# Attention steps on one core: the exponentials issued directly behind the maxima

## The chip, the cores and the metric

One core of a Trainium2 chip runs the whole program. The metric is the device time of one execution in microseconds (us); the runs shown of the kernel before took 1231.6, 1232.68 and 1233.63 us, median 1232.68 us. The profile is of a further execution, with its own time.

## The reference

Three stages follow each other: block-causal attention over 4 batches, 8 heads, 576 positions and 64 columns, a routed mixture of 8 experts, and a dense mixture of 4 experts. Only the first is touched by the change. Cut to it:

```python
scores = scale * np.matmul(q, k.transpose(0, 1, 3, 2))
scores = np.where(block_i >= block_j, scores, -1000000000.0)
scores = scores - np.max(scores, axis=-1, keepdims=True)
attn = np.exp(scores)
attn = attn / (np.sum(attn, axis=-1, keepdims=True) + 1e-09)
out = np.matmul(attn, v)
...
h = np.maximum(xc[mask] @ w1[e], 0.0)
y[mask] = gate_w[mask, None] * (h @ w2[e])
```

## The kernel before

**Units, groups, steps.** The attention is cut into 8 units (one batch, four heads). A unit has ten groups, and one step works on one group, so a unit has steps 0 to 9, and the attention has 80 (then a tail without exponentials). Query row tiles are rt 0 (64 rows) and rt 1 to 4 (128 rows). In units 0 to 6 the groups are: step 0 rt 0, step 1 rt 1, steps 2 and 3 rt 3 (two heads each), steps 4 and 5 rt 2, steps 6 and 7 rt 4 (heads 0 and 1), steps 8 and 9 rt 4 (heads 2 and 3). Unit 7 takes them in another order (`R7`).

**The order of a step** is written out by hand in `ORD`: each letter is a small function of `attention`, called once a step. As the scheduling is manual, the order in which the functions issue instructions is the order in which each engine takes them; engines are coupled by semaphores alone. The letters:

- S: TensorE makes the scores of the *next* group into a PSUM tile `s` (pool `ps_s`, three buffers, line 280).
- M: VectorE takes the negated row maxima `m` of this group (line 289).
- E: ScalarE turns the scores into exponentials `E` (line 296); it reads `s` and `m`. It issues nothing else. When an item is complete it also puts the item on the lists `turns` and `pvs`, with the step from which it is due (`TL`, `LG`).
- D: two pieces of the operand preparation of the next unit (`split_unit`): on ScalarE the scaled `kr` (line 209), `kh` (210) and `QH` (203), in steps 1, 2 and 3; the differences on GpSimd.
- R: the gate logits of finished rows (copies `xT`, line 397, and `lgs`, line 408, on ScalarE) and the routing of a batch of row tiles (`route`: a dozen small VectorE operations, one exponential on ScalarE, line 445).
- T: the exponentials are turned (`turn`). For rt 0, 2 and 4 ScalarE copies them to `HL` in 16 bits (line 328), GpSimd makes the rest (329) and SyncE issues a transposing DMA. For rt 1 and 3 (`PE_2`) TensorE transposes into a tile `tp` of the same three-buffer pool as the scores (line 322); one step later ScalarE copies it to `eT` (line 324) and VectorE subtracts that copy (line 325). These three ScalarE copies fall into steps 4, 5 and 6 of a unit.
- V: VectorE divides results by their sums (lines 362 to 365).
- P: TensorE's products with the values (lines 354 to 356).
- U, O: loads, and other small work.

ScalarE's work of a step is therefore, before the change: D, R, T, E. VectorE's is M, D, R, T, V in both kernels.

Of the kernel before, what the change touches and what calls it, by code (L numbers as in the profile page):

```python
# [52 lines left out]
class Kernel:  # L53
# [21 lines left out]
    SPE = ("AV", "AV", "AV", "AV", "AV", "AV", "AV", "AV")  # L75
    SB = 3
    PU, W2, X2 = 4, 1, 2
    ORD = "OSMDRTVPUE"
    TL = (2, 2, 2, 2, 2, 2, 2, 1, 3, 1, 1, 3, 0, 4, 2, 2)
    LG = (8, 9, 10, 9, 10, 4, 10, 9, 5, 12, 6, 9, 4, 4, 12, 2)  # L80
    SN = 2
# [430 lines left out]
    def attention(self, scored):  # L512
# [115 lines left out]
        while s < ns or turns or pvs or evs or self.routes or self.preps or side:  # L628
            self.tail = s >= ns
            for x in self.ORT if self.tail else self.ORD:  # L630
                order[x]()
# [533 lines left out]
```

## Time and profile before

| | |
|---|---|
| median of 3 runs | 1232.68 us (1231.6 to 1233.63) |
| profiled execution: time, span | 1235.5 us, 1233.9 us |
| TensorE busy, mean granted clock | 1130.4 us (92%), 0.960 |
| ScalarE busy | 510.7 us (41%) |
| VectorE busy | 824.8 us (67%) |
| GpSimd busy | 602.7 us (49%) |

The table is over the whole span. The attention is only its first part: its first exponential starts at 11.8 us, and its last ones are done at 201 us. In the profile DVE is VectorE, ACT is ScalarE, PE is TensorE, PEld its weight loads, POOL is GpSimd. A row of the timeline has a start, a duration, and in square brackets the time for which the engine had stood idle, with what ended that. A duration includes the time until the write is acknowledged; the next instruction on the same engine starts a little before that.

### The profile page before, as it was taken

The numbers are of one execution on the slowest core, as the hardware profiler recorded it, in microseconds if no ns is written. First come the engines' busy times: TensorE is split into PE (matmuls) and PEld (weight loads), VectorE is DVE, ScalarE is ACT, GpSimd is POOL, SyncE is SP. The second block draws the span as 40 slices with busy tenths as digits, with TensorE's granted clock in tenths as the row PEclk, the third lists the DMA queues.
The fourth block names the chain that finished last, engine by engine and source line by source line (L and its number), as shares of the span: only waits on it lengthen the run. The fifth ranks groups of instructions, "written<-read, shape, count | busy, mean of one in ns | idle before, by whom it ended". The sixth has DMA issues, their size and how long they took to land.

```text
span 1233.9 us, 21146 instructions
## 1 busy us (share of the span) xinstructions
PE 1130.4 (92%) x8105; PEld 1009.7 (82%) x8105; DVE 824.8 (67%) x1312; ACT 510.7 (41%) x900; POOL 602.7 (49%) x597
## 2 busy tenths in 40 slices
PE   5888888669898789999999999999899999999998
PEld 4778887558797678999889989888788888888887
DVE  5667576576425677766677666677877767767675
ACT  5877775356424552323322323324423332233321
POOL 6968784100011065544554454546655555555552
PEclk8889899689999989999999999999999999999999
DMA  5988749799524342111111111112311111111101
GB/s 182 208 184 195 181 116 210 254 316 312 194 92 150 100 127 69 35 35 48 39 47 39 35 35 52 35 52 69 120 35 54 50 52 52 35 52 52 35 1 69
DMA packets 129882, 123.89 MB, mean 100 GB/s; under 512 B 65965, under 2 KB 98733, under 8 KB 129744
## 3 DMA queue, kind: packets, MB, share of 16 engines
q1 hardware_dynamic: 127024, 117.48, 33.1%
q0 software_dynamic: 2720, 4.64, 1.2%
q8 instruction: 79, 1.29, 0.5%
q14 instruction: 59, 0.48, 0.1%
HBM read 91.83 MB, written 19.43 MB: 90 GB/s over the span
## 4 chain that ended last, share of the span: by engine, by line
PE 45%; DVE 9%; issue 8%; DMA 5%; ACT 4%; POOL 2%; POOLq 0%; another core or an unknown queue 0%; SPq 0%; DVEq 0%; ACTq 0%
PE yp L660 9%; PE yp L662 9%; PE yp L661 8%; PE hp L661 6%; PE hp L662 6%; PE hp L660 6%; DMA xi<-XS 4%; DVE acc L980 4%; DVE tl L893 2%; ACT hh L925 2%; DVE C L918 2%; ACT vh L889 1%; POOL C L918 1%; DMA XN<-ys,xg 1%; POOL p L918 1%
## 5 line engine op out<-in xcount | busy, mean ns | idle before, releaser
L925 ACT ACTIVATE hh<-C 128x512 fp32r<-128x512 f32 (+1 forms) x128 | 87.8, 686 | 433.6 <-DVE C L918 368.8
L660 PE MATMUL yp<-vh,hh 128*128 128x512 f32 x576 | 228.9, 397 | 10.9 <-ACT hh L925 10.9
L980 DVE SCALAR_TENSOR_TENSOR acc<-yp,p,acc 128x512 f32<-128x512 f32 x270 | 196.7, 742 | 56.6 <-PE yp L662 56.6
L662 PE MATMUL yp<-vh,hl 128*128 128x512 f32 x576 | 227.8, 395 | 0.3 <-DVE hl L926 0.3
L661 PE MATMUL yp<-vl,hh 128*128 128x512 f32 x576 | 228.0, 396 | 0.0
L926 DVE SCALAR_TENSOR_TENSOR hl<-C,hh 128x512 fp32r<-128x512 f32 (+1 forms) x128 | 120.9, 945 | 116.7 <-ACT hh L925 116.7
L918 POOL TENSOR_TENSOR p<-u,p 128x384 f32<-128x384 f32 (+1 forms) x64 | 60.3, 942 | 203.5 <-ACT p L915 203.5
L662 PEld LDWEIGHTS yp<-vh,hl 128*128 128x128 f32 x576 | 108.4, 188 | 31.8 <-DVE hl L926 8.2
L660 PEld LDWEIGHTS yp<-vh,hh 128*128 128x128 f32 x576 | 109.1, 189 | 27.4 <-ACT hh L925 14.3
L918 POOL TENSOR_TENSOR C<-u,p 128x384 f32<-128x384 f32 (+1 forms) x64 | 53.3, 833 | 149.6 <-ACT p L915 96.7
L661 PEld LDWEIGHTS yp<-vl,hh 128*128 128x128 f32 x576 | 109.0, 189 | 12.3
L661 PE MATMUL hp<-xsl,th 128*128 128x256 f32 (+1 forms) x384 | 113.9, 297 | 0.0
L662 PE MATMUL hp<-xsh,tl 128*128 128x256 f32 (+1 forms) x384 | 113.7, 296 | 0.0
L660 PE MATMUL hp<-xsh,th 128*128 128x256 f32 (+1 forms) x384 | 113.6, 296 | 0.0
L915 ACT COPY p<-hp 128x256 f32<-128x256 f32 (+1 forms) x192 | 74.8, 389 | 92.9 <-PE hp L662 92.9
L918 DVE TENSOR_TENSOR C<-hp,p 128x256 f32<-128x256 f32 (+1 forms) x128 | 57.6, 450 | 52.9 <-POOL p L918 52.9
L896 POOL TENSOR_TENSOR vl<-r,vh 128x1024 fp32r<-128x1024 f32 x31 | 91.3, 2945 | 0.0
L730 POOL DMA_INDIRECT XN<-ys,xg x10 | 13.0, 1299 | 155.4 <-DVE ys L729 106.1
L893 DVE TENSOR_TENSOR tl<-t,th 128x512 fp32r<-128x512 f32 x32 | 87.0, 2719 | 0.8 <-ACT th L891 0.8
L329 POOL TENSOR_TENSOR HL<-E,HL 128x640 bf16<-128x640 f32 (+2 forms) x39 | 66.5, 1721 | 32.1 <-ACT HL L328 23.5
L296 ACT ACTIVATE E<-s,m 128x320 f32<-128x320 f32 (+4 forms) x160 | 76.0, 532 | 10.4 <-DVE m L289 9.5
L660 PE MATMUL hp<-xdh,dh 128*128 128x256 f32 (+1 forms) x256 | 76.6, 299 | 1.9 <-ACT xdh L845 1.2
(212 smaller groups left out, 3093.8 us busy)
## 6 DMA issues: line engine op xcount, KB each, us to landing
r<-in_w_dram SPq DMA_DIRECT2D x128, 512.0 KB, 4.9
XN<-x SPq DMA_DIRECT2D x18, 256.0 KB, 8.7
x<-XN SPq DMA_DIRECT2D x18, 256.0 KB, 3.1
vr<-in_v_dram SPq DMA_DIRECT2D x7, 640.0 KB, 7.2
xg<-XS SPq DMA_DIRECT2D x16, 257.0 KB, 4.5
out_dram<-acc SPq DMA_DIRECT2D x16, 256.0 KB, 2.0
qr<-in_q_dram SPq DMA_DIRECT2D x7, 576.0 KB, 6.0
kr<-in_k_dram SPq DMA_DIRECT2D x7, 576.0 KB, 6.0
```

Source lines behind the costliest of these rows:

```text
L296: nc.scalar.activation(e, views[j], AF.Exp, bias=m[:R, c:c + 1])
L329: (nc.vector if item[:2] in self.HV else nc.gpsimd).tensor_tensor(HL[:R, w:2 * w].bitcast(BF16), Et[:R, 0:w], HL[:R, 0:w], ALU.subtract)
L660: nc.tensor.matmul(out, lhsT=ah, rhs=bh, start=start, stop=False)
L661: nc.tensor.matmul(out, lhsT=ah, rhs=bl, start=False, stop=False)
L662: nc.tensor.matmul(out, lhsT=al, rhs=bh, start=False, stop=stop)
L893: V.tensor_tensor(tl[:, 0:2], t[:, 0:2], th[:, 0:2].bitcast(F32), ALU.subtract)
L896: P.tensor_tensor(vl, r2, vh.bitcast(F32), ALU.subtract)
L915: nc.scalar.copy(t, product(a, b))
L918: add = lambda e, o, x, y: e.tensor_tensor(o, x, y, ALU.add)
L925: nc.scalar.activation(hh[:, i:i + 2], C[:, i:i + 2], AF.Relu)
L926: V.scalar_tensor_tensor(hl[:, i:i + 2], C[:, i:i + 2], 0.0, hh[:, i:i + 2].bitcast(F32), ALU.max, ALU.subtract)
L980: nc.vector.scalar_tensor_tensor(a, yp, self.p[:, n, e:e + 1], a, ALU.mult, ALU.add)
```

## The change

One string: in a step the letter E moves from the last place to the place behind M. All functions stay as they are.

```diff
-    ORD = "OSMDRTVPUE"
+    ORD = "OSMEDRTVPU"
```

ScalarE's work of a step then has the order E, D, R, T. One item, rt 0 of unit 7, has a `TL` of 0; as E comes in front of T in its step now, its turning starts one step earlier.

## Rows read from the trace of the kernel before

**Rows 1.** Busy time by engine in two stretches (us from the span's start).

```profile
core 0: us, PE busy (x) PEld busy (x) DVE busy (x) ACT busy (x) POOL busy (x), PEclk, DMA share, GB/s
20.00:183.00 163.00, 140.09 (x1977) 130.58 (x1978) 108.27 (x234) 126.08 (x226) 129.47 (x102) 0.89 0.76 173
183.00:205.00 22.00, 19.63 (x365) 18.47 (x364) 16.21 (x43) 16.26 (x35) 12.87 (x11) 1.00 1.10 195
```

**Rows 2.** Groups by line, ScalarE, 20 to 183 us: busy, mean ns | idle before.

```profile
L296 ACT ACTIVATE E<-s,m 128x320 f32<-128x320 f32 (+4 forms) x128 | 61.9, 539 | 3.4 <-DVE m L289 2.5 <-DVE r L362 0.9
...
L324 ACT CAST eT<-tp 128x896 f16<-128x896 f32 (+1 forms) x21 | 18.4, 876 | 23.0 <-PE tp L322 23.0
...
L397 ACT COPY xT<-xTp 128x512 f32<-128x512 f32 x11 | 6.5, 591 | 0.9 <-PE xTp L394 0.9
L408 ACT COPY lgs<-lg 128x9 f32<-128x9 f32 x11 | 1.9, 169 | 6.4 <-PE lg L402 6.4
L445 ACT ACTIVATE rt<-rt 128x32 f32<-128x32 f32 (+1 forms) x2 | 0.5, 233 | 3.0 <-DVE rt L439 3.0
```

**Rows 3.** Waits of TensorE, 20 to 183 us: total, times, longest.

```profile
PE s L280 <- ACT E L296: 10.5, 8, 1.7
PE s L280 <- DVE eT L325: 5.5, 7, 1.3
PE tp L322 <- ACT E L296: 5.3, 9, 1.6
```

**Rows 4.** Timeline of ScalarE, steps 4 to 8 of unit 4.

```profile
116.22 0.80 ACT L324 CAST eT<-tp 128x768 f16<-128x768 f32 x1
116.90 0.96 ACT L296 ACTIVATE E<-s,m 128x320 f32<-128x320 f32 x2
...
119.71 0.91 ACT L324 CAST eT<-tp 128x896 f16<-128x896 f32 x1 [1.10 <-PE tp L322]
120.51 0.95 ACT L296 ACTIVATE E<-s,m 128x320 f32<-128x320 f32 x2
123.07 0.91 ACT L324 CAST eT<-tp 128x896 f16<-128x896 f32 x1 [1.61 <-PE tp L322]
123.88 0.73 ACT L328 CAST HL<-E 128x640 f16<-128x640 f32 x1
124.50 0.75 ACT L296 ACTIVATE E<-s,m 128x576 f32<-128x576 f32 x1
```

**Rows 5.** Timeline of VectorE over the same steps.

```profile
117.06 0.96 DVE L325 TENSOR_TENSOR eT<-tp,eT 128x768 bf16<-128x768 f32 x1 [1.58 <-ACT eT L324]
117.93 0.81 DVE L289 TENSOR_REDUCE m<-s 128x2 f32<-128x640 f32 x1
120.65 1.09 DVE L325 TENSOR_TENSOR eT<-tp,eT 128x896 bf16<-128x896 f32 x1 [1.90 <-ACT eT L324]
121.66 0.15 DVE L362 TENSOR_SCALAR r<-og 128x4 f32<-128x4 f32 x1
...
122.39 0.75 DVE L289 TENSOR_REDUCE m<-s 128x1 f32<-128x576 f32 x1
124.01 1.09 DVE L325 TENSOR_TENSOR eT<-tp,eT 128x896 bf16<-128x896 f32 x1 [0.87 <-ACT eT L324]
125.02 0.75 DVE L289 TENSOR_REDUCE m<-s 128x1 f32<-128x576 f32 x1
```

**Rows 6.** Timeline of VectorE around a routing batch, steps 0 and 1 of unit 4.

```profile
105.75 0.42 DVE L289 TENSOR_REDUCE m<-s 64x4 f32<-64x256 f32 x1
...
109.40 0.96 DVE L289 TENSOR_REDUCE m<-s 128x4 f32<-128x768 f32 x1
```

**Rows 7.** Timeline of ScalarE over the same steps.

```profile
106.10 1.15 ACT L328 CAST HL<-E 128x1152 f16<-128x1152 f32 x1
107.16 0.91 ACT L296 ACTIVATE E<-s,m 64x64 f32<-64x64 f32 x4
107.95 1.16 ACT L209 ACTIVATE kr<-kr 128x1152 f32<-128x1152 f32 x1
...
110.45 1.36 ACT L296 ACTIVATE E<-s,m 128x192 f32<-128x192 f32 x4 [0.87 <-DVE r L362]
```

**Rows 8.** Busy time in a stretch of unit 5 (columns as in rows 1).

```profile
142.00:148.00 6.00, 6.00 (x55) 5.92 (x55) 2.46 (x5) 1.92 (x4) 5.84 (x6) 0.50 0.92 275
```

**Rows 9.** Groups by line, TensorE, 142.6 to 144.2 us: seven transposes.

```profile
L322 PE MATMUL tp<-ident,E 128*128 128x128 f32 x7 | 1.7, 426 | 0.0
```

**Rows 10.** Groups by line, TensorE, 93.8 to 94.8 us: seven transposes.

```profile
L322 PE MATMUL tp<-ident,E 128*128 128x128 f32 x7 | 1.0, 280 | 0.2 <-ACT E L296 0.2
```

## The prediction

> **What bounds the kernel now.** The edit touches the 80 steps of the attention alone, so I read the busy time of that stretch before anything else: from 20 to 183 us, which is six and a half units, TensorE is busy for 140.1 of 163 us, GpSimd for 129.5, ScalarE for 126.1, VectorE for 108.3 [rows 1]. No engine is full; the stretch is paced by how they wait for one another. The only order that the edit changes is that of ScalarE, and its work stays the same. That gives a simple account: the moment at which ScalarE has done its work up to a given step moves by exactly as much as its idle time before that step changes. Its idle time is 163 − 126.1 = 36.9 us now.
>
> The groups by line say what it waits for: 23.0 us ahead of the copies from `tp` until TensorE has transposed, 6.4 ahead of `lgs` and 0.9 ahead of `xT`, also for TensorE, 3.4 ahead of exponentials and 3.0 ahead of the routing's exponential for VectorE [rows 2]. Together 36.7, so nearly all of the 36.9 is explained. The reader is to see that the exponentials themselves hardly wait (3.4 us for 128): their maxima are long done when ScalarE comes to them, as D, R and T stand in between. What they do is to wait behind other work; TensorE pays for that with 10.5 us ahead of scores and 5.3 us ahead of transposes, where a PSUM tile is free only after an exponential [rows 3].
>
> **The change part by part.** *What moves.* E issues nothing but ScalarE's activations, one to four a step. They pass the D, R and T work on ScalarE and nothing else: E has no DMA, and puts nothing on SP's or POOL's queue. Now every ScalarE copy of a step stands behind that step's maxima. Its wait for `m` is the wait that is added to those copies.
>
> *What is gained.* An exponential of step s starts up to one step's copies earlier, and so do the scores that take its PSUM tile. Of TensorE's waits, 10.5 + 5.3 = 15.8 us [rows 3] hang on that. But TensorE's time is gained for the end only if it paces the units. ScalarE's waits for TensorE, 23.0 + 6.4 + 0.9 = 30.3 us [rows 2], should go too, since an earlier E(4) and E(5) let the transposes of steps 4 and 5 start earlier. I take all 30.3 as gone.
>
> *What is added.* In steps 4, 5 and 6 ScalarE copies a `tp`, and VectorE, in its order M, T, V, subtracts that copy before it comes to the next step's maxima. Today ScalarE does E(s) meanwhile. After the change E(s) lies behind it, and the next thing on its queue is E(s+1), which needs M(s+1), which stands behind that subtraction. The clock times of unit 4 give the price, as VectorE's three pieces keep their lengths:
> - Step 4 to 5: ScalarE is free 116.90 [rows 4]; the subtraction starts 117.06, the maxima start 117.93 and take 0.81 [rows 5], and 0.03 more reaches ScalarE: 118.77. Wait 1.87 us.
> - Step 5 to 6: free 120.51 [rows 4]; subtraction 120.65, the division of V, maxima 122.39 + 0.75 [rows 5]: 123.17. Wait 2.66 us.
> - Step 6 to 7: the `HL` copy follows, so free only 124.50 [rows 4]; subtraction 124.01, maxima 125.02 + 0.75 [rows 5]: 125.80. Wait 1.30 us.
>
> That is 5.83 us a unit. Seven units have this pattern in the stretch; the first has no results to divide in step 5, which saves 122.39 − 121.66 = 0.73 [rows 5]. Sum 7 × 5.83 − 0.73 = 40.1 us.
>
> *Routing batches.* Two fall into the stretch. The routing's own wait of 3.0 us stays [rows 2]. In unit 4 its VectorE work stands between M(0) and M(1): M(1) ends 109.40 + 0.96 = 110.36, 4.19 us behind the end of M(0), 106.17 [rows 6]. ScalarE has E(0), issue to issue 107.95 − 107.16 = 0.79, and one `HL` copy, 1.06, to fill this after the change, and waits 2.34; now it has `kr` and `xT` as well and waits 0.87 [rows 7]. So +1.5, and I take the same for the other batch, an estimate: 0 to 3 us for each. The waits of exponentials that exist now, 3.4, turn into the ones counted here; only the 0.9 at the routing stays.
>
> *ScalarE's idle time after:* 40.1 + 3.0 + 0.9 + 3.0 = 47.0 us, against 36.9: **10.1 us later** at 183 us.
>
> *What is behind that.* From 183 to 205 us TensorE is busy for 19.6 of 22 us [rows 1]. It enters this stretch with less unfinished work when ScalarE is late, so it can win back something between nothing and its 2.4 us of idle time; I take 1.5. Everything after the attention (routing of the last rows, weights, both mixtures) follows from its end, and I shift it unchanged. GpSimd's copies from `HL` and `QH` come about a microsecond later in their step; their results are needed several steps on, and it has 33.5 us free [rows 1], so I cost this at nothing; were GpSimd to fall behind, products would wait, at up to about 1 us a unit (an estimate, from the size of an exponential group). The early turning of rt 0 in unit 7 moves one small copy by one step: nothing, within 0.5 us either way.
>
> **Sum:** 10.1 − 1.5 = +8.6 us. The profiled execution took 1235.5 us, so 1244.1 for its like; it lies 2.8 us above the median of the runs. On the median, 1232.7 + 8.6 = 1241.3 us.
>
> **The rivals.**
> *TensorE sets the pace, and it gets faster.* It is the busiest engine [rows 1], and its waits for exponentials come where one reuses a score tile. If the 15.8 us [rows 3] are all gained, 1216.9 us; half, 1224.8. It decides if VectorE's subtraction and maxima don't hold ScalarE up for longer than TensorE did: the point lies at 36.9 / 7 = 5.3 us a unit with all waits counted, and the three new ones alone are 5.83. So it needs TensorE's gain to shorten VectorE's pieces, which are bare durations; against it. In a sentence apart: the Trainium skill, Perfetto Trace Analysis, section Optimization Strategy, says that consistent bubbles on the engine that should be saturated can mean that there isn't enough PSUM for the next tile, which would have one free the score tiles earlier, as this change does. Here the gaps do repeat, but the rule leaves out who pays for the earlier release. 17%.
> *No change.* The chain costs what it costs, yet routing adds nothing and the tail wins back its 2.4 us: 47.0 − 3.0 − 36.9 − 2.4 = +4.7; with a third of the 5.83 hidden by work that I have put too early, below zero. So within 2.5 us, around 1233. That includes the case in which the order of issue does not decide what waits, against which stands that VectorE's rows follow the letters exactly [rows 5]. 14%.
> *Slower still, through TensorE's clock.* In unit 5 six microseconds ran at a granted 0.50, the lower of the two levels, 1.2 GHz [rows 8], and seven transposes took 1.7 us there [rows 9] instead of 1.0 [rows 10]. TensorE had stood idle shortly before. With the new waits it idles in more places; if 0.7 to 1.4 us a unit (one or two such groups) comes onto the path, seven units give 5 to 10 us more: about 1248.5. In a sentence apart: the Trainium skill, TensorE: Matmul & The Clock Gate, Part 1, says that throttled is the default state and that activity releases it; the rows agree in direction. 15%.
>
> **How the numbers follow.** The forecast as worked out has 54%, slower still 15%, no change 14%, faster 17%. A difference of 0.2% is 2.5 us, about what a measurement of this kernel can tell from no change; so slower 0.69, same 0.14, faster 0.17. The predicted time is 1241.3 us. The forecast's own range is 1235 to 1247, from the routing terms (0 to 6 in place of 3), the tail (0 to 2.4) and GpSimd's bound. The range over the cases leaves out the better half of the faster one and the far end of the slower one: 1229 to 1253 us.
>
> **What would show it.** Right: behind the copies of steps 4, 5 and 6 the exponentials carry idle times of about 1.9, 2.7 and 1.3 us that end with VectorE's maxima, some 40 us in all; the copies from `tp` wait for TensorE hardly at all instead of 23.0; TensorE's 10.5 us ahead of scores shrinks, and its busy share still falls; the attention ends 8 to 10 us later and every later stage is shifted as a whole. Wrong: ScalarE's idle time up to the first exponential of unit 7 does not grow; or it grows and the end does not move, which would put the pace after the attention elsewhere (on the weights' DMA).

## The result, and where the time went

The changed kernel took 1244.13 us (median of 4, 1243.07 to 1246.69), beside 1232.14 us for the kernel before: a ratio of 1.010 (95% interval 1.008 to 1.0121), 12 us slower. The forecast was 1241.3 us, range 1229 to 1253. The profiled execution has a span of 1245.1 us, 11.2 more than before.

The steps to look at first are those of [rows 4]. The timeline of ScalarE of the changed kernel, steps 4 to 7 of unit 4:

```profile
128.36 0.80 ACT L324 CAST eT<-tp 128x768 f16<-128x768 f32 x1
130.92 0.95 ACT L296 ACTIVATE E<-s,m 128x320 f32<-128x320 f32 x2 [1.76 <-DVE m L289]
...
132.22 0.93 ACT L324 CAST eT<-tp 128x896 f16<-128x896 f32 x1
135.71 0.74 ACT L296 ACTIVATE E<-s,m 128x576 f32<-128x576 f32 x1 [2.56 <-DVE m L289]
136.35 0.90 ACT L324 CAST eT<-tp 128x896 f16<-128x896 f32 x1
137.13 0.74 ACT L328 CAST HL<-E 128x640 f16<-128x640 f32 x1
139.07 0.74 ACT L296 ACTIVATE E<-s,m 128x576 f32<-128x576 f32 x1 [1.20 <-DVE m L289]
```

The copies from `tp` no longer wait, and behind each of them the exponential waits for VectorE. The three idle times recur in every unit (in the first, without a division, they are 1.82, 1.82 and 1.20); over the seven units they are 38.0 us. That ScalarE's account as a whole changed as thought, but by more, is seen in its groups, 20 to 197.7 us (the last figure is the start of unit 7, which was 183.5 us before):

```profile
L296 ACT ACTIVATE E<-s,m 128x320 f32<-128x320 f32 (+4 forms) x128 | 61.0, 537 | 49.8 <-DVE m L289 45.9 <-DVE r L362 2.9 <-POOL HL L329 0.9
...
L324 ACT CAST eT<-tp 128x896 f16<-128x896 f32 (+1 forms) x21 | 18.4, 878 | 0.0
...
L397 ACT COPY xT<-xTp 128x512 f32<-128x512 f32 x11 | 6.5, 595 | 0.0
L408 ACT COPY lgs<-lg 128x9 f32<-128x9 f32 x11 | 1.9, 172 | 0.0
L445 ACT ACTIVATE rt<-rt 128x32 f32<-128x32 f32 (+1 forms) x2 | 0.5, 234 | 1.4 <-DVE rt L439 1.4
```

Set beside [rows 2]: waits of copies for TensorE 23.0 + 0.9 + 6.4 became 0.0; waits of exponentials 3.4 became 49.8. Some 12 us of the latter stand outside the three places. Examples from unit 4: step 1 (behind a routing batch), step 4, steps 8 and 9 (no wait), and step 0 of unit 5:

```profile
117.89 1.36 ACT L296 ACTIVATE E<-s,m 128x192 f32<-128x192 f32 x4 [2.89 <-DVE r L362]
...
127.52 0.95 ACT L296 ACTIVATE E<-s,m 128x320 f32<-128x320 f32 x2 [2.22 <-DVE m L289]
...
140.38 1.38 ACT L296 ACTIVATE E<-s,m 128x576 f32<-128x576 f32 x2
...
144.11 0.91 ACT L296 ACTIVATE E<-s,m 64x64 f32<-64x64 f32 x4 [0.81 <-DVE m L289]
```

Up to unit 7 the exponentials of step 0 wait 3.5 us in all (and the first of unit 7 another 1.5), those of step 9 never.

Stages, by busy time in windows (columns as in rows 1), changed kernel: the attention up to unit 7, unit 7 up to the last exponential, from there to the first weight copy of the first mixture, and, behind a gap of some 10 us, that mixture.

```profile
20.00:197.70 177.70, 146.99 (x1981) 134.11 (x1980) 110.23 (x234) 124.98 (x226) 129.63 (x102) 0.87 0.70 159
197.70:220.20 22.50, 19.52 (x261) 18.33 (x260) 11.93 (x28) 14.55 (x31) 10.02 (x9) 0.78 1.07 202
220.20:242.00 21.80, 16.59 (x305) 15.54 (x302) 14.10 (x72) 7.07 (x20) 9.42 (x13) 0.89 0.93 266
251.80:449.80 198.00, 167.68 (x1036) 147.87 (x1036) 112.05 (x128) 99.51 (x135) 20.67 (x21) 0.94 0.61 204
```

The same stages of the kernel before, from unit 7 on:

```profile
183.50:201.50 18.00, 16.34 (x281) 15.18 (x279) 12.49 (x29) 14.12 (x31) 9.66 (x8) 1.00 1.13 197
201.50:228.00 26.50, 19.61 (x278) 17.91 (x278) 14.17 (x72) 6.28 (x19) 9.43 (x13) 0.78 0.99 253
238.00:439.00 201.00, 168.55 (x1036) 148.40 (x1036) 112.21 (x128) 99.50 (x135) 21.54 (x21) 0.92 0.61 201
```

Unit 7 begins 14.2 us later and takes 4.5 us more, so the attention ends 18.7 us later; then 4.7 us come back in the tail and 3.0 in the first mixture. 14.2 + 4.5 − 4.7 − 3.0 = 11.0, and the stretches not shown add 0.2, which makes the span's 11.2. The first number behind the last bracket is the granted clock: from unit 7 on, where a stage gains or loses, it has moved too (1.00 to 0.78, 0.78 to 0.89, 0.92 to 0.94).

### The profile page after: what moved, and what is told of

It reads as the page before. It is cut to its first block, busy times and chain, and to the rows that moved or that the text cites. A ratio compares the mean times of both kernels' runs of the same rounds, so it can differ in the third digit from the quotient of the medians.

```text
span 1245.1 us, 21148 instructions
## 1 busy us (share of the span) xinstructions
PE 1136.3 (91%) x8105; PEld 1013.3 (81%) x8105; DVE 825.7 (66%) x1312; ACT 510.0 (41%) x900; POOL 601.4 (48%) x597
## 4 chain that ended last, share of the span: by engine, by line
PE 46%; DVE 9%; issue 5%; ACT 4%; POOL 2%; DMA 0%; SPq 0%; POOLq 0%; DVEq 0%; ACTq 0%
PE yp L660 9%; PE yp L662 9%; PE yp L661 8%; PE hp L661 6%; PE hp L662 6%; PE hp L660 6%; DVE acc L980 3%; DVE tl L893 2%; ACT hh L925 2%; DVE C L918 2%; ACT vh L889 1%; POOL C L918 1%; POOL p L918 1%; PE tp L839 1%; PE yp L721 0%
## 5 line engine op out<-in xcount | busy, mean ns | idle before, releaser
L660 PEld LDWEIGHTS yp<-vh,hh 128*128 128x128 f32 x576 | 109.1, 189 | 27.4 <-ACT hh L925 14.3
```

The costliest lines, as they stand in the source:

```text
L660: nc.tensor.matmul(out, lhsT=ah, rhs=bh, start=start, stop=False)
```

## Experiments

Executions are compared by their ratio to the kernel before on the same chip; a ratio is given in us of 1232. A profile is of one execution, and executions of one kernel differ by up to 16 us (1236.4 to 1252.0 in one run below), so the stages of a profile and the median over executions can differ; where they do, both are given. Theory A is the prediction's: exponentials wait for maxima that stand on VectorE behind the subtraction of a copied tile. Theory B: what costs is that operand copies and logits now come later, behind the exponentials. Theory C: TensorE's stalls and its lower clock behind them.

**The copy steps alone, and all others alone.** In the loop of steps, with `ORD` as changed and `ORC` as before:

```diff
-    for x in self.ORT if self.tail else self.ORD:
+    at = (s % 10 in (4, 5, 6) and s < 70 or s in (76, 79))
+    for x in self.ORT if self.tail else self.ORC if at else self.ORD:
```

> Exponentials stand last again in the steps that copy a turned tile from PSUM (steps 4, 5, 6 of units 0 to 6, and the two such steps of unit 7), directly behind the maxima in all others. Theory A (ScalarE waits there for maxima that stand behind VectorE's subtraction): the three waits of 1.76, 2.56 and 1.20 us go, 38 us in all, the copies wait for TensorE's transposes again (23 us before), and what is left of the 12 us are the waits at the first exponential of a unit and at routing, some 3 us: 1232 to 1238 us. Theory B (the loss comes from operand copies and logits that now stand behind the exponentials, in all steps): two thirds or more of the loss stay, 1240 us or more.

The second swaps the two orders.

> The complement of the run above: exponentials directly behind the maxima only in the steps that copy a turned tile, last in all others. Theory A: the three waits are all there, 38 us against 23 to 30 us of waits for TensorE that go, so 6 to 12 us slower than before: 1238 to 1244 us. Theory B: these are 23 of 80 steps, without operand copies, so under 3 us: 1232 to 1235 us.

Measured: last at the copies 1.0076 (1.0052 to 1.0099), +9.4 us; first at the copies alone 1.0017 (0.9997 to 1.0038), +2.1 us. Both lie where theory B was put and not where theory A was, so taken alone they speak for B; the runs further down tell against it. The groups of ScalarE (columns as in rows 2), for the run with the early exponentials at the copies alone, 20 to 189.2 us, then for its complement, 20 to 190.5 us:

```profile
L297 ACT ACTIVATE E<-s,m 128x448 f32<-128x448 f32 (+4 forms) x129 | 61.2, 536 | 37.1 <-DVE m L290 35.1 <-DVE r L363 0.9 <-POOL HL L330 0.8
...
L325 ACT CAST eT<-tp 128x896 f16<-128x896 f32 (+1 forms) x21 | 18.4, 877 | 0.0
```

```profile
L297 ACT ACTIVATE E<-s,m 128x320 f32<-128x320 f32 (+4 forms) x128 | 61.7, 537 | 17.8 <-DVE m L290 14.1 <-DVE r L363 2.9 <-POOL HL L330 0.6
...
L325 ACT CAST eT<-tp 128x896 f16<-128x896 f32 (+1 forms) x21 | 18.3, 874 | 21.9 <-PE tp L323 21.9
```

With early exponentials at the copies alone, ScalarE's idle time from 20 us to the start of unit 7 grows from 37.3 us (163.5 us, busy 126.2) to 42.9: the exponentials wait 33.3 us more (37.1 against 3.8), 23.0 us of copies and 6.3 us of logits are gone, and the rest are small changes. Unit 7 begins 5.7 us later in this profile. In the complement the exponentials wait 17.8 us, the copies still wait 21.9, and unit 7 begins 7.0 us later. So in the profiles the two kinds of steps share the delay almost evenly, while by the medians most of the cost lies outside the copy steps. The profiled execution at the copies alone was the slowest of its ten, 1240.65 us against a median of 1236.35. That exponentials wait for maxima stands; how the loss divides between the two kinds of steps is not settled. The two medians together, 11.5 us, come close to the whole.

**The division out of the way.**

```diff
-    ORD = "OSMEDRTVPU"
+    ORD = "OSMEDRVTPU"
```

> The changed kernel with VectorE's divisions (V) ahead of the turned tiles (T) in a step. Theory A: in step 5 the division (0.74 us) leaves the way between the subtraction and the next maxima, so that wait falls from 2.56 to 1.82 us in six units, 4.4 us in all: 1239 to 1241 us. If TensorE's clock or the order of ScalarE's copies set the loss: no change beyond 1 us, 1243 to 1245 us.

Measured 1.0122 (1.0083 to 1.016), +15 us, outside both ranges. The waits ahead of step 6 fell from 17.2 to 13.4 us over the units, as theory A has it, and unit 7 began 1.3 us earlier than in the changed kernel. But the stretch from the last exponential to the first weight copy took 30.8 us instead of 21.8, at a granted clock of 0.61 instead of 0.89:

```profile
218.80:249.60 30.80, 25.11 (x305) 23.25 (x302) 14.22 (x72) 7.04 (x20) 9.45 (x13) 0.61 0.63 183
```

So 9 us of this profile come from the tail; why its clock was lower there, no run shows. A total alone could not have told that the wait had shrunk.

**Exponentials in front of the turned tiles only.**

```diff
-    ORD = "OSMEDRTVPU"
+    ORD = "OSMDRETVPU"
```

> Exponentials behind operand preparation and routing, but in front of the turned tiles: they pass T alone. Theory A: the three waits stay, shortened only where a copy of logits fills them (about half a microsecond a unit); the waits at routing and at the first exponentials of a unit shrink: 1239 to 1243 us. Theory B: the passed operand copies are back in front, so the time is that of before, 1232 to 1235 us.

Measured 1.0070 (1.0036 to 1.0104), +8.6 us, where theory A said (1236.4 to 1252.0 us over ten executions). Operand copies and logits are back in front, and most of the loss remains, which tells against theory B.

**Which of the other steps.** The same edit of the loop with early exponentials in steps 9, 0 and 1, then in 9 and 0, then in 1 alone:

> Exponentials directly behind the maxima in steps 9, 0 and 1 of units 0 to 6 only, last in all others. In the run with the copies' steps excluded these steps held 10 us of new waits (divisions of two results and the second half of a routing batch ahead of the maxima), with little removed. Theory A, widened: 4 to 8 us slower than before, 1236 to 1241 us. If those waits are only TensorE's lateness seen from ScalarE: within 2 us of before.

> Exponentials directly behind the maxima in steps 9 and 0 of units 0 to 6 only. The run with steps 9, 0 and 1 was 0.68% slower and held 5.5 us of waits at step 9 and 3.7 at step 0 (maxima behind divisions that wait for TensorE's products), of which the 4.3 us of waits of logits copies that went are to be taken off: by theory A 3 to 6 us slower than before. If the routing batch at step 1 makes the loss: within 2 us of before.

> Exponentials directly behind the maxima in step 1 of units 0 to 6 only (in front of kr and of the logits copy). Theory A: one routing batch stands in front of the maxima of step 1, 2.9 us against 0.9 before, nothing else changes: 1 to 4 us slower than before. Theory C (the stall at that batch starts a stretch at half clock whatever ScalarE does): as before within 2 us, or the same 4 us in unit 4 with and without.

Measured: 1.0068 (1.0044 to 1.0092), +8.4 us; 1.0046 (1.0023 to 1.0069), +5.7 us; 1.0008 (0.9987 to 1.0029), no difference. Step 1, where `kr` and the logits copy are passed and a routing batch stands on VectorE, costs nothing that can be measured by itself (−1.6 to 3.6 us); that is what theory C had, it leaves theory A's 1 to 4 us open, and it tells against theory B. By the medians steps 9 and 0 hold most of it. The profile of the run with steps 9 and 0 does not show that loss: its execution took 1232.95 us, against a median of 1239.02, and unit 7 begins 1.2 us later than before. It does show the waits. ScalarE in it, steps 8 and 9 of unit 4 and step 0 of unit 5:

```profile
129.09 0.75 ACT L297 ACTIVATE E<-s,m 128x576 f32<-128x576 f32 x1 [0.59 <-DVE m L290]
130.91 0.74 ACT L297 ACTIVATE E<-s,m 128x576 f32<-128x576 f32 x1 [1.07 <-DVE m L290]
131.55 0.58 ACT L398 COPY xT<-xTp 128x512 f32<-128x512 f32 x1
132.02 1.16 ACT L329 CAST HL<-E 128x1152 f16<-128x1152 f32 x1
134.00 0.91 ACT L297 ACTIVATE E<-s,m 64x64 f32<-64x64 f32 x4 [0.81 <-DVE m L290]
134.80 1.15 ACT L329 CAST HL<-E 128x1152 f16<-128x1152 f32 x1
```

Before, the `HL` copies stood in front of these two exponentials and covered the time until the maxima were made. In step 0 VectorE comes to them only behind the divisions of two results. The timeline of VectorE in the changed kernel, around step 0 of unit 5, shows what it waits for there itself:

```profile
141.53 0.16 DVE L362 TENSOR_SCALAR r<-og 128x4 f32<-128x4 f32 x1 [1.17 <-PE og L356]
...
142.87 0.15 DVE L362 TENSOR_SCALAR r<-og 64x4 f32<-64x4 f32 x1 [0.51 <-PE og L356]
...
143.61 0.41 DVE L289 TENSOR_REDUCE m<-s 64x4 f32<-64x256 f32 x1
```

TensorE's products of step 8 come last, then two divisions, then the maxima, then the exponential, which waits 0.81 us there (144.11). Over the whole stretch up to unit 7 the divisions wait longer for products than before (kernel before, 20 to 183.5 us, then changed kernel, 20 to 197.7):

```profile
L362 DVE TENSOR_SCALAR r<-og 128x4 f32<-128x4 f32 (+1 forms) x31 | 4.7, 153 | 3.9 <-PE og L356 3.9
L362 DVE TENSOR_SCALAR r<-og 128x4 f32<-128x4 f32 (+1 forms) x31 | 4.7, 152 | 11.4 <-PE og L356 11.3
```

The waits at step 9, though, belong to the runs with early exponentials in a few steps: in the changed kernel step 9 has none, so the 5.7 us are not a part of its loss as they stand.

**Maxima one step ahead.** This moves the maxima out from behind that work, with both places of the exponentials:

```diff
 def maxima():
-    if s < ns:
-        next(scs[s])
+    for j in range(2) if s == 0 else (s + 1,):
+        if j < ns:
+            next(scs[j])
```

> The changed order, but VectorE makes the maxima one step ahead (of the group whose scores TensorE has just been given), so that they stand in front of the turned tiles, routing and divisions of the step before. Theory A, widened by the runs so far (the exponentials pay for whatever stands on VectorE between a step's copies and the next maxima: subtractions in steps 4 to 6, divisions and routing in steps 9, 0 and 1): nearly all of the 52 us of waits of exponentials go, the gain of the early exponentials is kept, 1224 to 1234 us. Theory C (TensorE's stalls at routing and its half clock behind them make the loss, and the waits only mirror them): 1240 us or more.

> The kernel before, with the maxima one step ahead on VectorE and nothing else. Exponentials wait for maxima for 3 us only before, so there is little to win: 1230 to 1236 us by both theories. It tells what the other order on VectorE is worth by itself, to set beside the run with both edits.

Measured: with early exponentials 1.0045 (1.0012 to 1.0079), +5.5 us; with late ones 1.0083 (1.0051 to 1.0116), +10.2 us. Neither is where it was expected, but the four corners speak together. With the maxima in place, early exponentials cost 12 to 13 us; with the maxima ahead they cost nothing, and rather save (1238.39 against 1242.5 us; the two intervals overlap a little). ScalarE's idle time from 20 us to unit 7 says the same, in one profile each: with the maxima in place it grows from 37.3 to 52.7 us with early exponentials, with the maxima ahead it falls from 50.2 to 40.5. So it is the place of the maxima that makes early exponentials dear. What I had not priced is VectorE. Its groups, run with early exponentials, 20 to 185.3 us:

```profile
L289 DVE TENSOR_REDUCE m<-s 128x1 f32<-128x576 f32 (+3 forms) x66 | 53.8, 815 | 54.1 <-PE s L280 50.1 <-ACT E L296 2.0 <-ACT HL L328 1.7
L325 DVE TENSOR_TENSOR eT<-tp,eT 128x896 bf16<-128x896 f32 (+1 forms) x21 | 21.8, 1038 | 2.5 <-ACT eT L324 2.5
```

It now waits 50.1 us for scores (10.4 in the kernel before; 54.4 with the maxima ahead and late exponentials), with subtractions, routing and divisions queued behind, and the exponentials still wait 34.8 us in all. The wait went one engine further back.

**The changed kernel again.**

> The changed kernel itself on this chip, beside the runs above: 0.8 to 1.2% slower than the kernel before, by both theories. It gives the sum that the parts are to be set against.

Measured 1.0108 (1.0077 to 1.0139), +13.3 us. The stages of its profile repeat those of the first: unit 7 begins at 199.5 us and takes 23.0, the tail takes 21.3 and the first mixture 198.3.

**TensorE kept busy behind a routing batch.**

```diff
-    for c in range(4):
+    for c in [0, 1, 2, 3] * (3 if self.fill and not self.tail else 1):
         nc.tensor.transpose(tp[:, c], xs[:, c * 128:(c + 1) * 128], self.ident)
+    self.fill = False
```

`route` sets `fill` when it has issued its products; the transposes overwrite the tile with the same values.

> The changed kernel, with the four transposes of a row tile made three times over (same tile, same values) in the step after a routing batch has used TensorE, which is where TensorE stood idle for 1.8 and 2.2 us for VectorE's part of the routing. Eight more transposes for each of two batches, some 1.1 us each time, inside that idle time. Theory C: TensorE's clock then does not fall in unit 4 (mean 0.78 in the changed kernel), unit 4 becomes 2 to 4 us shorter, and the time with it: 1240 to 1242 us. Theory A: unit 4 stays as long within 1 us, 1243 to 1246 us.

> The control: the same added transposes in the kernel before. Its unit 4 ran at a mean clock of 0.93, so by both theories within 2 us of the kernel before.

Measured: changed and filled 1.0150 (1.0118 to 1.0182), +18.5 us; before and filled 0.9964 (0.9939 to 0.9990), 4.4 us faster, 12 executions against 29. Both totals lie outside what any theory had. Unit 4 in windows (columns as in rows 1), in the changed kernel and in the changed and filled one; the third row is the latter's stretch from the last exponential to the first weight copy:

```profile
113.00:144.10 31.10, 25.93 (x326) 23.86 (x324) 18.77 (x42) 19.62 (x36) 23.11 (x21) 0.78 0.69 142
```

```profile
113.90:144.70 30.80, 24.65 (x332) 22.63 (x330) 18.79 (x41) 19.68 (x36) 23.08 (x21) 0.89 0.70 143
221.00:251.40 30.40, 23.56 (x305) 21.90 (x302) 13.91 (x72) 7.03 (x19) 9.40 (x13) 0.67 0.65 192
```

The mean clock of unit 4 rose from 0.78 to 0.89. With two levels, 1.0 and 0.5, time at the lower one is twice the missing share: 2 × 0.22 × 31.1 = 13.7 us before the filling, 2 × 0.11 × 30.8 = 6.8 us with it. The unit got 0.3 us shorter. That is what theory A had for unit 4, and not the 2 to 4 us of theory C. In the profile of the changed kernel again unit 4 took 32.2 us at 0.73; so over three executions from 0.73 to 0.89 its length moves by 1.4 us, against the 6.3 us that it lost to the change. The clock is at most a small part of the loss there. The loss of the filled run against the changed kernel lies in its tail, 30.4 us against 21.8 at 0.67 against 0.89, as in the run with the divisions in front; all six of its executions (1247.98 to 1255.30 us) are slower than all eight of the changed kernel, though on another chip, and why transposes added in the attention should do that to the tail, no run shows.

## Why the prediction was right, and where it was not

The direction and the mechanism held: exponentials that stand early wait for maxima behind other work of VectorE, and ScalarE's idle time sets when unit 7 starts. From 20 us to that start it grew from 37.3 us to 177.7 − 125.0 = 52.7, by 15.4 us; the busy time in the stretch is 1.2 us smaller, and unit 7 starts 14.2 us later. The forecast for that point was 10.1. The sizes of the terms held only in part.

- *The three waits.* Forecast 1.87, 2.66 and 1.30 us; measured 1.76, 2.56 and 1.20. I had counted from the start of the row that came next, the profile counts from the end of the row before, 0.1 us later (116.22 + 0.80 = 117.02 against 116.90 [rows 4]). 38.0 us against 40.1.
- *Waits for TensorE gone.* Forecast all 30.3; measured 0.0 left. Held.
- *The price of the two together.* 40.1 − 30.3 = 9.8 us in the sum, 38.0 − 30.3 = 7.7 in the changed kernel's rows. In the run with the copy steps alone it is 2.1 us by the median (−0.4 to 4.7) and 5.7 at the start of unit 7 by the profile. The term was too large rather than too small; by how much is open.
- *All other waits of exponentials* were the term that was mis-sized. The sum had 0.9 left of the old 3.4, and 3.0 for routing; the rows have 11.8, and 1.5 more ahead of the first exponential of unit 7. Of these, 2.89 stand behind the routing in unit 4 (forecast 2.34), 2.22 in step 4 of unit 4 (where VectorE's division in front of the maxima had waited 3.29 us for products), and 5.0 at the first exponentials of units. The last two had no term at all: I had listed VectorE's order as M, D, R, T, V and followed V into the next maxima in step 5 alone, but it stands in front of them wherever a result is complete, behind TensorE's last products. The routing's own wait fell to 1.4, where 3.0 was to stay.
- *Where it is lost.* The three waits stand alike in every unit, some 5.5 us, but 10.5 of the 14.2 us are lost in units 3 and 4 (27.4 and 31.1 us, before 23.2 and 24.8). In unit 3 the copies had waited only 1.7 us that could go, half the mean of the seven, and unit 4 holds the 2.89 and the 2.22.
- *Behind the attention.* Forecast −1.5 us and then a shift. Measured +4.5, −4.7 and −3.0: the attention ended 18.7 us later and not 8 to 10, and the later stages were not shifted as a whole. That the errors up to there were partly undone in the tail and the first mixture was no part of the sum, so that the total came so close is in part luck. Over the runs the tail took from 20.2 us at a clock of 0.96 to 30.8 at 0.61; that the clock makes its length is argued, not shown.
- *The rivals.* TensorE did not set the pace; its waits for scores, 10.5 us, were to shrink and stayed at 9.7, while the early exponentials waited 49.8 us themselves. Its lower clock was there (0.87 in the stretch against 0.89), but in unit 4, where it was as low as in any (0.78), it was at most a small part of the loss.

Left open: how the loss divides between copy steps and the others, and why the parts with early exponentials in steps 2, 3, 7 and 8 and in unit 7 add about 1 us (9.4 − 8.4), which no run resolves.

## What to carry to other kernels

On an in-order engine an instruction that seems to be kept waiting by others may be using them as cover: before it is moved forward, read what the *releasing* engine does between its last result and the one needed now, through all of its letters, not only the one in view. Where a wait is moved from one engine to another, price the new one in its own place and then test the places apart: here three waits that could be computed to a tenth of a microsecond were for the most part paid for by the waits that went, and scattered ones that were not looked for cost about as much as what was left. Read a run's stages before its total, since a stage behind the one under test can move by more than the effect.

## What was not expected

Eight added transposes at each of two places made the kernel *before* faster, by 0.36% (0.10 to 0.61%): 1228.02 us, the fastest of all kernels here; within 2 us was expected. In its profile units 4 to 6 ran at full clock throughout, beside 0.93, 0.87 and 0.93 before, and took 23.6, 23.6 and 23.1 us beside 24.8, 26.8 and 24.7. The two runs in windows, kernel before first:

```profile
107.20:132.00 24.80, 21.70 (x319) 20.16 (x318) 17.57 (x42) 19.70 (x37) 21.61 (x21) 0.93 0.73 159
132.00:158.80 26.80, 23.94 (x344) 22.57 (x345) 16.31 (x38) 19.51 (x39) 18.32 (x13) 0.87 0.83 188
158.80:183.50 24.70, 21.39 (x302) 19.96 (x299) 17.48 (x45) 19.31 (x37) 22.28 (x23) 0.93 0.45 113
```

```profile
106.70:130.30 23.60, 21.70 (x337) 20.38 (x335) 17.75 (x42) 19.66 (x38) 20.63 (x20) 1.00 0.71 160
130.30:153.90 23.60, 20.73 (x343) 19.41 (x345) 16.78 (x38) 19.46 (x39) 19.76 (x14) 1.00 1.06 222
153.90:177.00 23.10, 20.66 (x310) 19.27 (x307) 17.38 (x45) 19.26 (x36) 20.70 (x22) 1.00 0.49 118
```

That the clock is the whole of this gain is argued, not shown: it is one profile of twelve executions, and units without any added transposes were faster in it too (1.3 us over units 0 to 3). The run with early exponentials in step 1 alone, as fast as the kernel before and without added transposes, had units 5 and 6 at full clock as well, in 23.7 and 23.6 us. It would fit that in the kernel before TensorE's time does count, as copies wait for it there, while in the changed one they do not (23.0 us against 0.0).
